# One half of the scores copied by VectorE in five steps of a batch (attention with mixed heads, then a Fourier mixer)

## Chip, core and metric

The program runs on one core of a Trainium2 chip. The core has TensorE (PE in the profile; its weight loads are PEld), VectorE (DVE), ScalarE (ACT), GpSimd (POOL) and SyncE (SP, which here only issues DMA transfers). The metric is the time of the whole program on the device, in microseconds; the median of the runs is used.

## The reference

Two blocks follow each other, all in float32. Only the first is touched by the change, the second is named because its work goes on beside it.

```python
scores = scale * np.matmul(q, k.transpose(0, 1, 3, 2))      # 8 batches, 12 heads, 448 x 448
scores = np.einsum('bhij,hg->bgij', scores, w_pre)          # heads mixed
attn = np.exp(scores - max) / (sum + 1e-09)                 # softmax over j
attn = np.einsum('bhij,hg->bgij', attn, w_post)             # heads mixed again
x = np.matmul(attn, v)                                      # then (B, H, S, D) -> (B, S, H*D)
u = x + np.real(np.fft.fft(np.fft.fft(x, axis=1), axis=2))
un = (u - mean) / sqrt(var + 1e-06)
out = u + np.maximum(un @ w_ch1, 0.0) @ w_ch2
```

## The kernel before

The program has a mixing stage (attention and the Fourier transforms, `mix_phase`) and a feed-forward stage (`ffn_phase`), which starts while the last batch's transforms are still being done.

**Steps.** The mixing stage is a software pipeline of 184 steps, 23 for each of the 8 batches (`GS`). A batch's 448 query rows are cut into 8 blocks of two or three steps (`BLOCKS`). A step mixes and normalises 20 query rows for all 12 heads. For the step two ahead it runs the premix on TensorE (`emit_premix`, L656, into the two `mx` banks), row maxima on VectorE (L663), two exponentials on ScalarE (L670), sums and reciprocals on VectorE (L677, L678) and a scaling on GpSimd (L680). For the step itself it runs the postmix on TensorE (L690) and a transpose on VectorE (L703).

**Products beside the steps.** These are due at fixed steps, given by tables at the top of the file:
- `emit_qk` (L628): the scores of two heads (of rows x = 0 and 1) for one block, into two `ms` banks. Six slices make up a block's tile `Sb`. Due by `AT_QK`.
- `emit_av` (L720): attention times v, two `ms` banks.
- "full" products: `emit_xpose` (L601; here also called a turn: seven transposes of q or k, four into one `ms` bank and three into the next), `emit_x` (L764, transposes of the result X, two banks), `emit_z` (L829) and `emit_s2` (L845), the two passes of the Fourier transform, one bank each. The last one is followed by four additions on VectorE (L856, L858) that read its bank.

All of them share four `ms` banks in strict rotation. A bank is free again once it has been copied into SBUF. These copies all go through one helper (`copy`, L489), which picks ScalarE for "a" and VectorE for "d". For scores the table says `"QK": "aa"`, both halves by ScalarE; only the first two blocks of the first batch have `"ad"`.

**Order.** Each engine's instruction order in this stage is written out by hand for TensorE, VectorE, ScalarE and GpSimd (`manual_schedule`). Within a step it follows `ORDERS`, alternating:

```python
"pre post flush AV max0 exp0 QK max1 exp1 turn scale conv full gather"
"pre post flush max0 max1 QK exp0 AV turn exp1 scale conv gather full flush"
```

A product puts its copies on a list `pend`; they are written into the queues at the next `flush`, and every "full" product begins with one (`take`). So the score copies of a step that has a full product come, on each engine, behind that step's `exp1`, `scale` and `conv`. `conv` is one weight-conversion operation on VectorE (`wts.deal(1)`, lines 250 to 310), a chore that prepares the feed-forward weights from step 4 on.

A gather (L645) then collects twelve heads' rows for a step out of `Sb` into `Kr`. It is issued by SP, waits for the block's last score copy, and is due five steps ahead of its step. `Sb` has two buffers, so the first score copy of a block waits until the gathers of the block before the last are done.

**Steps that matter below**, counted within a batch (step number modulo 23), with what TensorE does behind the scores there: step 0 (L845, then L764), step 2 (a second pair of scores, then L845), step 5 (L764, then a turn of q), step 13 (L764, then a turn of q), step 15 (a turn of q, then a turn of k). In step 5, 13 and 15 the turns belong to the next batch, so the last batch has none; there VectorE has statistics for the feed-forward stage in their place.

Of the kernel before, what the change touches and what calls it, by code (L numbers as in the profile page):

```python
# [43 lines left out]
NBL = len(BLOCKS)  # L44
BLOCK_AT = [sum(k[2] for k in BLOCKS[:n]) for n in range(NBL + 1)]
GS = BLOCK_AT[-1]
# [47 lines left out]
AT_QK = ((0, 2, 1), (0, 1, 2), (0, 1, 2), (1, 2, 2),  # L94
         (0, 1, 2), (0, 1, 2), (0, 1, 2), (0, 1, 2))
AT_AV = ((1, 2, 4), (0, 1, 3), (1, 3, 5), (1, 3, 4))
AT_X = ((13, 0), (23, 1), (28, 3), (29, 2))
AT_Z = (39, 40, 40, 42)
AT_S = ((42, 44), (46, 48))
# [7 lines left out]
ENG = {("tr", "q", 4): "d", ("tr", "q", 3): "a", ("tr", "k", 4): "a",  # L107
       ("tr", "k", 3): "d", "QK": "aa", "AV": "aa", "X": "aa", "z": "a"}
# [342 lines left out]
def mix_phase(ctx, tc, rest, ident, q, k, v, w_pre, w_post, u_scr, u_rev, wts, lead):  # L451
# [36 lines left out]
    def copy(eng, out, in_):  # L488
        (nc.scalar.copy if eng == "a" else nc.vector.tensor_copy)(out=out, in_=in_)  # L489
# [11 lines left out]
    def ms_tile():  # L501
        return ms[-1]()
# [54 lines left out]
    def emit_load_qk(b, xx, nm, y):  # L557

        src = q if nm == "q" else k
        if y == 0 and b == 0 and xx == START[-1]:  # L560

            if "raw" not in first:
                first["raw"] = ppv.tile([P, GT, 2 * S], F32, name="Pv", tag="Pv")
            batches[b]["raw" + nm, xx] = first["raw"][:, nm == "q"].rearrange(
                "p (c x d) -> p c x d", c=C7, x=2)
        elif y == 0:
            batches[b]["raw" + nm, xx] = praw.tile([P, C7, 2, D], F32, name="raw" + nm,
                                                   tag="raw")
        t = batches[b]["raw" + nm, xx]
        for x in range(2):  # L570
            eng = nc.gpsimd if b else (nc.sync, nc.scalar if xx == START[0] else nc.gpsimd)[x]
            eng.dma_start(
                out=t[64 * y:64 * y + 64, :, x, :],
                in_=src[b, 6 * y + 2 * xx + x].rearrange("(p c) d -> p c d", c=C7))
        return True

    def emit_load_v(b, pr, y):
        if y == 0:
            batches[b]["v", pr] = pvv.tile([P, 2, C7 * D], F32, name="vv", tag=f"vv{pr}")
        h = 6 * y + 2 * pr  # L580
        nc.gpsimd.dma_start(
            out=batches[b]["v", pr][64 * y:64 * y + 64, :, :],
            in_=v[b, h:h + 2].rearrange("h (p c) d -> p h (c d)", c=C7))


    def emit_xpose(b, xx, nm):
        st = batches[b]
        raw = st.pop(("raw" + nm, xx))
        w = WQ if nm == "q" else S
        t = pqt.tile([P, 2, w], F32, name=nm + "T", tag=nm + "T")  # L590
        st[nm + "T", xx] = t
        rt = _row(t)
        if nm == "q":
            eng = nc.gpsimd if b else nc.vector
            eng.memset(t[:, :, 0:MG], 0.0)
            eng.memset(t[:, :, MG + S:WQ], 0.0)
        evs = []
        for c0, n in ((0, 4), (4, 3)):
            ps = ms_tile()
            for c in range(n):  # L600
                nc.tensor.transpose(  # L601
                    ps[:, c * P:(c + 1) * P],
                    raw[:, c0 + c].rearrange("p x d -> p (x d)"), ident[:, :])
            if nm == "q":
                dst = _ap(t, MG + c0, [[rt, P], [1, n], [WQ, 2], [C7, 64]])
                src = ps[:, :n * P].rearrange("p (c y t) -> p c y t", c=n, y=2)
            else:
                dst = _ap(t, 32 * c0, [[rt, P], [32, n], [HS, 4], [1, 32]])
                src = ps[:, :n * P].rearrange("p (c y t) -> p c y t", c=n, y=4)
            evs.append(lambda dst=dst, src=src, n=n: copy(ENG["tr", nm, n], dst, src))  # L610
        return evs

    def emit_qk(n, xx):

        bk = blocks[n]
        st = batches[bk["b"]]
        engs = ENG["QK"] if n > 1 else "ad"
        if "Sb" not in bk:
            bk["Sb"] = psb.tile([P, 6, S], F32, name="Sb", tag="Sb")
        c0, w = bk["r0"] + MG, R * bk["rs"]  # L620
        n = 64 + w
        pss = [ms_tile() for _ in range(2)]
        for y in range(2):
            for o in (64 * y, 64 * y + 32):
                lo = c0 + o - 64 + (0 if y else w)
                hi = min(lo + 32, c0 + w)
                for x in range(2):
                    nc.tensor.matmul(  # L628
                        pss[x][o:o + hi - lo, :S],
                        st["qT", xx][64 * x:64 * x + 64, y, lo:hi],  # L630
                        st["kT", xx][64 * x:64 * x + 64, y, :],
                        start=True, stop=True)
        return [lambda x=x: copy(engs[x], bk["Sb"][:n, 2 * xx + x, :],
                                 pss[x][:n, :S]) for x in range(2)]
# [250 lines left out]
    def due(kind, at, fn):  # L885
        fill[kind].append((at, len(fill[kind]), fn))
# [4 lines left out]
    for b in range(B):  # L891
        f = b * GS
        at_t = [(a, nm, xx) for xx, at in enumerate(AT_T) for nm, a in zip("qk", at)]
        if b == 0:

            for i, xx in enumerate(START):
                for j, nm in enumerate("kq"):
                    for y in range(2):
                        due("none", -40, lambda xx=xx, nm=nm, y=y: emit_load_qk(0, xx, nm, y))
                    due("full", 2 * i + j - 20, lambda xx=xx, nm=nm: emit_xpose(0, xx, nm))  # L900
                for n, at in enumerate((2 * i - 18, i - 13)):
                    due("QK", at, lambda n=n, xx=xx: (emit_qk(n, xx), n))
            for pr in range(3):
                for y in range(2):
                    due("none", -40, lambda pr=pr, y=y: emit_load_v(0, pr, y))
        else:
            for at, (a, nm, xx) in zip(AT_L if b > 1 else AT_L1, sorted(at_t, key=lambda e: e[0])):
                for y in range(2):
                    due("none", f + at[y] - GS if b > 1 else at[y],
                        lambda b=b, xx=xx, nm=nm, y=y: emit_load_qk(b, xx, nm, y))  # L910
            for xx, at in enumerate(AT_T):
                for nm, a in zip("qk", at):
                    due("full", f + a - GS,
                        lambda b=b, xx=xx, nm=nm: emit_xpose(b, xx, nm))
        for pr in range(3 if b else 0):
            for y in range(2):
                due("none", f + AT_V[pr][y], lambda b=b, pr=pr, y=y: emit_load_v(b, pr, y))
        for n in range(0 if b else 2, NBL):
            for xx in range(3):
                due("QK", AT_QK0[n][xx] if b == 0 and n in AT_QK0 else  # L920
                    f + BLOCK_AT[n] - 8 + AT_QK[n][xx],
                    lambda n=NBL * b + n, xx=xx: (emit_qk(n, xx), n))
        for n in range(NG):
            for pr in range(3):
                due("AV", f + GROUP_AT[n + 1] + AT_AV[n][pr],
                    lambda a=b * NG + n, pr=pr: (emit_av(a, pr), None))
            at, gi = AT_X[n]
            if b == B - 1 and n > 1:
                at += 2
            due("full", f + at, lambda g=groups[b * NG + gi]: emit_x(g))  # L930
        for n, at in enumerate(AT_Z):
            due("full", f + at, lambda b=b, n=n: emit_z(b, n // 2, n % 2))
        for pair in range(2):
            for par in range(2):
                due("full", f + AT_S[pair][par],
                    lambda b=b, pair=pair, par=par: emit_s2(b, pair, par))
# [19 lines left out]
    def take(kind, s):  # L956
        large = 0
        while fill[kind] and fill[kind][0][0] <= s:
            fn = fill[kind].pop(0)[2]
            if kind == "none":  # L960
                large += bool(fn())
            elif kind == "full":
                flush()
                pend.extend((1, e, None) for e in fn())
            else:
                room(2)
                evs, n = fn()
                pend.extend((1, e, n) for e in evs)
        return large
# [3 lines left out]
    with tc.manual_schedule(engines={ET.PE, ET.DVE, ET.Activation, ET.Pool}):  # L973
        while s <= TOT - GS + AT_X[-1][0]:
            old = len(later)
            n = take("none", s)
# [577 lines left out]
```

## Time and profile before

| what | value |
|---|---|
| median of 3 runs | 2299.19 us (2297.72 to 2299.28) |
| profiled execution | 2299.42 us, its span 2297.6 us |
| granted TensorE clock | 0.998 |
| premix L656 on TensorE | 2944 matmuls, 192.2 us |
| scores L628 on TensorE | 3072 matmuls, 191.6 us |
| attention times v, L720 | 5376 matmuls, 160.8 us |
| maxima L663 on VectorE | 368, 618 ns each |
| transposes L703 on VectorE | 184, 1107 ns each |
| exponentials L670 on ScalarE | 368, 631 ns each |

The page counts busy time per engine, then follows the chain that ended last back from the last instruction. The mixing stage fills roughly the first 800 us. Every copy of a bank into SBUF has the line L489, whoever makes it, so copies are told apart by tile and engine: `Sb<-ms` is a score copy, `qT<-ms` and `kT<-ms` those of a turn, `X<-ms` those of L764, `XT<-ms` those of L720. In a timeline the columns are start, duration (both us), engine, line, operation, tiles, shapes and count; in brackets the idle time before it and what ended it. Copies in a row on one engine overlap a little, so two of them take less than twice the time of one.

### The profile page before, as it was taken

The page shows a single profiled execution, that of the slowest core. Times are in us where ns is not written, and L with a number is a line of the kernel's source. Part 1 is how long each engine was busy: PE and PEld are TensorE (multiplying, and loading weights), DVE is VectorE, ACT ScalarE, POOL GpSimd, SP SyncE. Part 2 cuts the span into 40 slices and gives each one's busy share as a digit, 9 for nine tenths or more (in the row PEclk, how much of TensorE's full clock was granted, in tenths as well). Part 3 has the DMA queues.
Part 4 walks back from the last instruction along what each step waited for, and adds up shares of the span by engine and source line. Part 5 has one row for each costly group of instructions (what it writes and reads, how often), then busy time and mean ns, then how long its engine had stood idle before and what let it go on. Part 6 is the DMA issues. An engine that isn't in the chain of part 4 may idle for free.

```text
span 2297.6 us, 60793 instructions
## 1 busy us (share of the span) xinstructions
PE 2249.2 (98%) x22894; PEld 1740.7 (76%) x22894; DVE 1711.2 (74%) x3640; ACT 1167.1 (51%) x3330; POOL 1292.1 (56%) x1805
## 2 busy tenths in 40 slices
PE   7999999999999999999999999999999999999998
PEld 3455555555554677777899999999999899999998
DVE  5778787888877757776877787778778777765545
ACT  4676767767676533231445445444444445434434
POOL 7677878879768541221555555546555645454334
PEclk9999999999999999999999999999999999999999
DMA  7566565666756475649677887788787987795664
GB/s 185 168 178 181 168 192 171 190 179 181 202 151 190 143 265 182 230 162 327 191 181 180 252 214 184 212 195 242 204 197 184 277 188 174 191 257 121 143 146 76
DMA packets 228063, 439.45 MB, mean 191 GB/s; under 512 B 35964, under 2 KB 149558, under 8 KB 227772
## 3 DMA queue, kind: packets, MB, share of 16 engines
q1 hardware_dynamic: 156620, 301.52, 38.2%
q0 software_dynamic: 68864, 133.00, 30.4%
q8 instruction: 183, 3.00, 0.6%
q10 hardware_dynamic: 2288, 1.05, 0.2%
q14 instruction: 108, 0.88, 0.1%
HBM read 213.16 MB, written 143.16 MB: 155 GB/s over the span
## 4 chain that ended last, share of the span: by engine, by line
PE 87%; DVE 5%; DMA 3%; ACT 2%; issue 1%; POOL 1%; SPq 1%; ACTq 0%; DVEq 0%; POOLq 0%
PE psP L1213 18%; PE psP L1335 14%; PE psR L1213 9%; PE psR L1335 7%; PE mx L656 6%; PE ms L720 6%; PE ms L628 5%; PE po L690 5%; PE psQ L1213 4%; PE psQ L1335 3%; PE psP L1290 3%; PE ms L845 2%; PE ms L601 2%; DMA Kr<-Sb 1%; PE psR L1290 1%
## 5 line engine op out<-in xcount | busy, mean ns | idle before, releaser
L1369 POOL DMA_DIRECT2D out_dram<-od x172 | 209.1, 1276 | 261.7 <-DVE od L1357 175.3
L680 POOL TENSOR_SCALAR PP<-PP,rcp 128x448 f32<-128x448 f32 x368 | 234.6, 647 | 170.2 <-DVE rcp L678 123.8
L670 ACT ACTIVATE PP<-mx,nmx 128x448 f32<-128x448 f32 x368 | 230.2, 631 | 165.2 <-DVE nmx L663 157.2
L663 DVE TENSOR_REDUCE nmx<-mx 128x1 f32<-128x448 f32 x368 | 212.5, 618 | 101.2 <-PE mx L656 99.1
L1176 POOL TENSOR_TENSOR hq<-h 128x128 f32<-128x128 f32 (+1 forms) x210 | 130.0, 619 | 255.9 <-ACT h L1235 122.3
L1363 ACT COPY od<-psP 128x192 f32<-128x192 f32 x488 | 156.1, 320 | 172.0 <-PE psP L1335 170.6
L1366 DVE TENSOR_TENSOR od<-od 128x768 f32<-128x768 f32 x210 | 201.3, 972 | 52.7 <-ACT od L1363 52.3
L703 DVE STREAM_TRANSPOSE Pv<-po 128x896 f32<-128x896 f32 x184 | 203.7, 1107 | 2.9 <-PE po L690 2.1
L489 ACT COPY Sb<-ms 124x448 f32<-124x448 f32 (+1 forms) x378 | 181.7, 540 | 46.0 <-PE ms L628 19.2
L656 PE MATMUL mx<-Kr,kw 60*32 60x448 f32 x2944 | 192.2, 549 | 4.3 <-ACT PP L670 2.3
L628 PE MATMUL ms<-kT,qT 64*32 64x448 f32 (+1 forms) x3072 | 191.6, 545 | 3.9 <-ACT qT L489 2.8
L720 PEld LDWEIGHTS ms<-Pv,vv 64*64 64x64 f32 x5376 | 138.1, 132 | 73.7 <-issue 48.8
L690 PE MATMUL po<-PP,kw 60*32 60x448 f32 x2944 | 184.0, 537 | 1.2 <-POOL PP L680 1.1
L1213 PE MATMUL psP<-qs,w1t 128*128 128x256 f32 x744 | 179.2, 380 | 2.4 <-DVE h L1234 1.5
L1213 PE MATMUL psP<-ks,w1t 128*128 128x256 f32 x744 | 179.3, 380 | 0.4 <-DVE h L1234 0.3
L720 PE MATMUL ms<-Pv,vv 64*64 64x120 f32 (+1 forms) x5376 | 160.8, 263 | 3.6 <-ACT Sb L489 2.2
L254 POOL TENSOR_SCALAR wst<-wst 128x256 f32<-128x256 f32 (+1 forms) x76 | 118.6, 1569 | 67.2 <-ACT wst L265 66.9
L1213 PEld LDWEIGHTS psP<-qs,w1t 128*128 128x128 f32 x744 | 139.5, 190 | 19.4 <-DVE h L1234 1.9
L1213 PEld LDWEIGHTS psP<-ks,w1t 128*128 128x128 f32 x744 | 139.5, 190 | 17.2 <-DVE h L1234 0.7
L1213 PE MATMUL psP<-ub,w1t 128*128 128x256 f32 x528 | 127.2, 379 | 1.1 <-DVE h L1234 1.1
L1234 DVE TENSOR_TENSOR h<-h,psP 128x512 f32<-128x512 f32 x42 | 28.8, 686 | 127.9 <-PE psP L1213 112.3
L1335 PE MATMUL psP<-w2t,hq 128*128 128x192 f32 x490 | 122.5, 332 | 1.2 <-DVE od L1357 1.2
(199 smaller groups left out, 5301.6 us busy)
## 6 DMA issues: line engine op xcount, KB each, us to landing
Kr<-Sb SPq DMA_DIRECT2D x730, 105.0 KB
out_dram<-od POOLq DMA_DIRECT2D x172, 384.0 KB, 6.3
qs<-ub SPq DMA_DIRECT2D x89, 384.0 KB
ks<-ub SPq DMA_DIRECT2D x88, 384.0 KB
ub<-ub SPq DMA_DIRECT2D x79, 384.0 KB
w1t<-w SPq DMA_DIRECT2D x42, 384.0 KB
w2t<-w SPq DMA_DIRECT2D x42, 384.0 KB
raw<-in_moe_w_ch_dram SPq DMA_DIRECT2D x32, 384.0 KB
```

The source lines that it names most:

```text
L628: nc.tensor.matmul(pss[x][o:o + hi - lo, :S], st["qT", xx][64 * x:64 * x + 64, y, lo:hi], st["kT", xx][64 * x:64 * x + 64, y, :], start=Tr ...
L656: nc.tensor.matmul(mx[x][64 * z + o:64 * z + o + 32, :S], kw1[64 * x:64 * x + KR, o:o + 32], Kr[64 * x:64 * x + KR, z, :], start=True, sto ...
L663: nc.vector.tensor_reduce(nmx[:, :], steps[T]["mx"][x][:, :S], axis=AX.X, op=ALU.max, negate=True)
L670: nc.scalar.activation(steps[T]["PP"][:, x, :], steps[T]["mx"][x][:, :S], ACTF.Exp, bias=steps[T]["nmx", x][:, :], accum_out=steps[T]["den ...
L680: nc.gpsimd.tensor_scalar(PP[:, x, :], PP[:, x, :], rcp[:, x:x + 1], 1.0, op0=ALU.mult, op1=ALU.mult)
L690: nc.tensor.matmul(po[o:o + 32, z, :S], kw2[64 * z:64 * z + KR, y, :], PP[64 * z:64 * z + KR, :, c * HS:(c + 1) * HS], start=True, stop=True)
L703: nc.vector.transpose(turned[a]["Pv"][:, j, :].rearrange("p (z s) -> p z s", z=2), steps[T]["po"][:, :, :S])
L720: nc.tensor.matmul(pss[y][64 * x:64 * x + 64, :nu * R], st["v", pr][64 * y:64 * y + 64, x, jb * D:(jb + 1) * D], _ap(Pv, 64 * y * rp + 32 ...
L1213: mm = nc.tensor.matmul(p[:, m, :], w1[i][:, kc, m * P:(m + 1) * P], ub[:, kc, :], start=i in (0, 4, 1)[:3 - seed] and m == kc == 0, stop= ...
L1335: nc.tensor.matmul(ps[j, key][:, :DQ], a, b, start=m in (0, 4), stop=True, skip_group_check=True)
L1366: eng.tensor_tensor(D[j][:, :, :], D[j][:, :, :], D[k][:, :, :], op=ALU.add)
L1369: nc.gpsimd.dma_start(out=acc[t, r, d], in_=D[j][:, :, :], accum_op=ALU.add)
```

## The change

In the steps 0, 2, 5, 13 and 15 of a batch (`TWO`), the second of the two score copies (x = 1) is put on VectorE. The step is worked out from the tables where the product is made due, and handed to `emit_qk`. The first batch's blocks 0 and 1 keep what they had. Step 2 makes two score products, so it has two such copies; the other steps have one. Nothing else is edited.

```diff
+TWO = (0, 2, 5, 13, 15)
...
-    def emit_qk(n, xx):
+    def emit_qk(n, xx, at=None):
...
-        engs = ENG["QK"] if n > 1 else "ad"
+        engs = "ad" if n < 2 or at in TWO else ENG["QK"]
...
             for xx in range(3):
                 due("QK", AT_QK0[n][xx] if b == 0 and n in AT_QK0 else
                     f + BLOCK_AT[n] - 8 + AT_QK[n][xx],
-                    lambda n=NBL * b + n, xx=xx: (emit_qk(n, xx), n))
+                    lambda n=NBL * b + n, xx=xx, at=(BLOCK_AT[n] - 8 + AT_QK[n][xx]) % GS:
+                    (emit_qk(n, xx, at), n))
```

## The prediction

> **What bounds the kernel now.** I read the page first, then the view of one source line (L489, the helper that makes every bank copy), then the waits of the mixing stage, and last the timeline of one changed step.
>
> ```profile
> PE 2249.2 (98%) x22894; PEld 1740.7 (76%) x22894; DVE 1711.2 (74%) x3640; ACT 1167.1 (51%) x3330; POOL 1292.1 (56%) x1805
> ...
> PE 87%; DVE 5%; DMA 3%; ACT 2%; issue 1%; POOL 1%; SPq 1%; ACTq 0%; DVEq 0%; POOLq 0%
> ```
>
> TensorE bounds it: 87% of the chain that ended last. VectorE is the next busiest (74%), ScalarE has half its time free. Time is won or lost only where a bank copy makes TensorE wait, so the copies come next:
>
> ```profile
> L489 ACT COPY Sb<-ms x378: 524/538/610, 13.0 to 758.9; 124x448 f32<-124x448 f32 x165, 104x448 f32<-104x448 f32 x24
> ...
> L489 DVE COPY Sb<-ms x6: 625/625/625, 13.0 to 27.2; 124x448 f32<-124x448 f32 x6
> ...
>   PE ms L601: 7.3, 20
> ```
>
> A score copy takes 0.54 us on ScalarE and 0.625 us on VectorE. The last line is from the list of who waited for the copies: TensorE's turns of q and k (L601) stood still for 7.3 us in 20 places. The waits from 100 to 800 us add the other kind:
>
> ```profile
> PE ms L845 <- ACT Sb L489: 2.7, 6, 0.6
> ```
>
> So at most about 10 us of TensorE's time hang on score copies in the changed steps. Which half of the copies ends these waits is seen in step 5 of batch 5:
>
> ```profile
> 531.12 1.10 DVE L703 STREAM_TRANSPOSE Pv<-po 128x896 f32<-128x896 f32 x1
> ...
> 531.90 0.20 ACT L670 ACTIVATION_READ_ACCUMULATOR PP<-mx,nmx 128x1 f32 x1
> 532.00 0.96 ACT L489 COPY Sb<-ms 124x448 f32<-124x448 f32 x2
> 532.11 0.99 POOL L790 TENSOR_TENSOR xs<-xs 113x383 f32<-113x383 f32 x1
> 532.21 0.16 DVE L677 TENSOR_REDUCE rcp<-den 128x2 f32<-128x4 f32 x1
> 532.40 0.17 DVE L678 RECIPROCAL rcp<-rcp 128x2 f32<-128x2 f32 x1
> 532.48 1.04 DVE L297 TENSOR_TENSOR wst<-wst,tmp 128x384 f32<-128x384 f32 x1
> ...
> 532.58 0.99 PE L601 MATMUL ms<-ident,rawq 128*128 128x128 f32 x7 [0.60 <-ACT Sb L489]
> ...
> 533.45 1.12 DVE L489 COPY qT<-ms 128x512 f32<-128x512 f32 x1
> 533.49 0.98 PE L656 MATMUL mx<-Kr,kw 60*32 60x448 f32 x16
> ```
>
> Single records give the rest: ScalarE's first copy runs from 532.00 to 532.52, the second ends at 532.96. With four banks in rotation, X (L764) takes the two that the scores don't hold, and the turn needs the scores' banks: four transposes into the first half's, three into the second half's. The turn starts 0.05 us after the FIRST copy ends; its fifth transpose follows 0.50 us later (533.08) without a stop. The wait is for the first copy, which comes right after the two exponentials. The second is never waited for.
>
> [...]
>
> **The change part by part.** 47 copies (39 of 124 rows, 8 of 104) leave ScalarE for VectorE; the comparison of the instruction orders shows nothing else moved on TensorE, ScalarE or GpSimd. Removed: 47 x 0.43 us (the distance of two copies in a row on ScalarE) = 20 us of an engine that is half idle. Added: 47 x some 0.54 us = 25 us on VectorE. The new copy goes behind the reciprocal and behind the weight chore (the "conv" entry; L297 above), in front of the turn's own VectorE copy. TensorE's fifth transpose now waits for VectorE instead of ScalarE; the first four wait for ScalarE's first copy as before, which moves nowhere.
>
> The cost of each turn is then: end of the chore + 0.54 us (VectorE instructions start about 0.08 us before the last one's end, 0.625 - 0.08) + 0.05 us (from a copy's end to TensorE's start, as above), less the time at which the fifth transpose started. Chore end / fifth transpose, in us, by batch:
> Step 5, batches 1 to 6: 147.12/146.93, 245.70/245.13, 342.19/341.75, 438.01/437.31, 533.52/533.08, 628.15/628.03. Late by 0.78 + 1.16 + 1.03 + 1.29 + 1.03 + 0.71 = 6.0.
> Step 13, batches 0 to 6: 88.88/89.19, 179.96/179.47, 277.15/277.47, 372.29/372.61, 469.01/468.84, 563.91/563.94, 659.58/659.64. Late by 0.28 + 1.08 + 0.27 + 0.27 + 0.76 + 0.56 + 0.53 = 3.8.
> Step 15, batches 0 to 6 without 3: 97.19/97.50, 188.56/188.05, 285.62/285.77, 477.15/477.14, 572.19/572.24, 667.69/667.94. Late by 0.28 + 1.10 + 0.44 + 0.60 + 0.54 + 0.34 = 3.3. In batch 3 the first copy itself waited for a gather until 380.88, when VectorE was free: nothing. Step 5 of batch 0 finds free banks: nothing. Batch 7 has no turns.
> Sum 13.1 us over 19 turns, all on TensorE's path: the next premix (L656) is right behind the turn.
>
> Step 0: the products behind (L845, then X) take the two free banks and the first copy's; no wait on VectorE. But the new copy stands ahead of the four additions (L856, L858) that free L845's bank, and step 1's first product needs it. In batches 4 to 7 they start 0.31, 0.29, 0.44 and 0.46 us later; against where L628 or L720 started (417.52, 512.82, 607.79, 703.61) that is 0.24 + 0.07 + 0.35 + 0.25 = 0.9 us.
> Step 2: two copies go, but L845 takes the bank of the first, which stays on ScalarE: its wait of 2.7 us stays. The two new ones end at 520.53 in batch 5, when VectorE idles until 520.62 for L845: hidden.
>
> VectorE's later start on the turn's copies does not come through: in batch 5 after step 5 they end at about 535.1, and the next maximum, which waits 1.0 us after the premix's start, is due at 534.52 + 1.0 = 535.5. On SP's queue the gather of a block waits for its last copy: in step 5 from 532.98 to about 534.1, but TensorE is 1.0 us later there itself, so the distance holds; in step 2 by 0.25 us, with three steps left until the premix that needs it. One store of u per batch goes one gather (0.8 us) later, with no one waiting for its tile then.
>
> Sum: 13.1 + 0.9 = 14.0 us. I take off 1 us for places where TensorE waits longer for other reasons than a turn's normal 0.23 us (gathers that arrive late, as in step 15 of batch 3): they can swallow a delay made shortly before. That leaves +13.0. The profiled execution took 2299.42 us (span 2297.6), hence 2312.4; its distance to the median 2299.19 is 0.2, hence 2312.2, taken as 2312.
>
> Bounds of what the trace does not show. A copy behind a chore may start earlier (the turn's k copy ends 0.39 us behind the q copy for 384 columns, so 0.45 for 448): 19 x 0.09 = 1.7 us less. From VectorE's end to TensorE's start may be 0.1 us: 1 us more. Swallowed: 0 to 4 us. Together +9 to +16.
>
> **Rivals.**
> 1. Forecast: the second half waits behind the chore; 2312 (2308 to 2316). For it: program order and the times above. 0.78.
> 2. Faster: ScalarE, freed of 0.43 us, gives back the waits of L601 and L845, 7.3 + 2.7 = 10 us: 2289. For it: these waits are put down to its score copies, and ScalarE's work in a step ends late. Against it: they end with the first copy. It decides if the first copy, or the exponentials ahead of it, came some 0.2 us earlier in most steps, and chores shrank to under 0.3 us so that nothing was given back. 0.06.
> 3. No change: later waits for gathers swallow most, say 11 of 14 us: 2302. Against it: such waits beyond the normal are about 4 us in the trace. 0.07.
> 4. Slower still: VectorE's extra 25 us push maxima and exponentials into the next premix, or late gathers hold up ScalarE's first copy of a block (it sat 18.6 us for gathers in 9 places). If half of the 25 us showed beside a part of the 14: 2320. Against it: room of 0.4 us and more in the steps worked above. 0.09.
>
> **How the numbers follow.** A difference under 0.2% (4.6 us) can't be told from none. Slower: 0.78 + 0.09, less a little for a forecast that is nearly swallowed: 0.86. Same: rival 3, 0.07. Faster: 0.07. The range: cases 1 and 4 up to 2319, down to 2304.
>
> **What would show it.** In the profile after, the fifth transpose of the turns in steps 5, 13 and 15 waits for "DVE Sb" for 0.3 to 1.3 us, some 13 us in all; waits of L601's first transpose on ScalarE stay near 0.23 us each; VectorE holds 53 score copies at about 625 ns; the premixes behind are late by as much and nothing makes it up. Wrong it would be if those transposes don't wait for VectorE, or if the mixing stage ends less than 5 us later.

## The result, and the profile after

| | before | after |
|---|---|---|
| median, measured side by side (6 runs each) | 2299.24 us (2292.60 to 2300.12) | 2312.61 us (2309.16 to 2317.68) |
| profiled execution, its span | 2299.42, 2297.6 us | 2309.16, 2307.4 us |
| score copies on ScalarE, on VectorE | 378, 6 | 331, 53 |
| mixing stage ends (last copy of L720's banks) | 798.0 us | 811.2 us |

The ratio is 1.0061, 95% interval 1.0048 to 1.0074: the changed kernel is slower, by 13.4 us as the difference of the medians. The profiled execution of the changed kernel is its fastest of six, so the two profiles lie only 9.8 us apart; the section on the prediction comes back to this. In the changed kernel a line of before has moved by 1, behind the step function by 2: L489 is now L490, L601 is L602, L764 is L765, and so on.

The engines' busy time and the engines' shares of the chain that ended last, from the page of the changed kernel:

```profile
PE 2251.6 (98%) x22894; PEld 1738.9 (75%) x22894; DVE 1732.6 (75%) x3687; ACT 1149.3 (50%) x3283; POOL 1291.0 (56%) x1805
...
PE 88%; DVE 5%; DMA 3%; ACT 1%; issue 1%; SPq 1%; POOL 1%; DVEq 0%; ACTq 0%; POOLq 0%
```

TensorE does the same work: 2251.6 us busy after 2249.2. VectorE has 21 us more, ScalarE 18 us less, and neither bounds the program. Of the 9.8 us between the two profiles, 7.4 are time in which TensorE stands, 2.4 come from its busy time. The view of the copies' line shows where it stands:

```profile
L490 ACT COPY Sb<-ms x331: 523/532/587, 13.3 to 772.3; 124x448 f32<-124x448 f32 x142, 104x448 f32<-104x448 f32 x24
L490 DVEq EVENT_SEMAPHORE  x158: 49/50/50, 41.4 to 768.2; - x158
...
L490 DVE COPY Sb<-ms x53: 604/623/626, 13.3 to 768.3; 124x448 f32<-124x448 f32 x45, 104x448 f32<-104x448 f32 x8
...
  PE ms L602: 15.6, 37
```

The columns of the first three are count, shortest, median and longest duration in ns, first and last start in us. The last line is from the list of who waited for these copies: 15.6 us in 37 places where the kernel before had 7.3 us in 20. I had not counted on the second line; it matters in the third experiment. The waits from 100 to 800 us split TensorE's standing by what ended it:

```profile
PE ms L602 <- DVE Sb L490: 10.2, 18, 1.1
PE ms L602 <- ACT Sb L490: 4.5, 15, 0.8
PE ms L846 <- ACT Sb L490: 2.3, 6, 0.7
```

The first line is new. The waits for ScalarE's first copy (second line; 6.5 us in 17 places before) and the wait of step 2 (third line; 2.7 us before) stayed about as they were. Step 5 of batch 5 once more, now in the changed kernel:

```profile
538.86 0.53 ACT L490 COPY Sb<-ms 124x448 f32<-124x448 f32 x1
...
539.27 0.17 DVE L679 RECIPROCAL rcp<-rcp 128x2 f32<-128x2 f32 x1
...
539.35 1.02 DVE L298 TENSOR_TENSOR wst<-wst,tmp 128x384 f32<-128x384 f32 x1
...
539.45 0.66 PE L602 MATMUL ms<-ident,rawq 128*128 128x128 f32 x4 [0.39 <-ACT Sb L490]
...
540.29 0.61 DVE L490 COPY Sb<-ms 124x448 f32<-124x448 f32 x1
...
540.96 0.55 PE L602 MATMUL ms<-ident,rawq 128*128 128x128 f32 x3 [0.85 <-DVE Sb L490]
```

ScalarE's one copy ends at 539.39 and the turn starts 0.05 us later, as before. Then the seven transposes, one group of before, are cut in two: the fifth comes at 540.96, 1.51 us after the first instead of 0.50. It waits for VectorE's copy, which started 0.08 us before the chore (L298) ended; from the copy's end to the transpose it is 0.06 us. (The bracket says 0.85 because it counts from the modelled end of the fourth transpose; that, and the two turns ahead of 100 us, is why the 10.2 us of the view above are less than the sum below.)

This distance from the first transpose to the fifth can be read from single records for every turn. From step 0 on it is 0.49 us in nearly every turn of the kernel before (0.44 to 0.52; the six turns ahead of step 0, at the start of the program, have 0.85 to 0.91). In the changed kernel it is 1.25, 1.65, 1.52, 1.77, 1.51, 1.69 in step 5 (batches 1 to 6), 0.91 in four turns of step 13 and 1.33, 1.06, 1.03 in the others, and 0.90 to 1.59 in step 15. Less 0.49 each, 20 turns are late by 6.45 + 3.63 + 3.93 = 14.0 us.

### The profile page after: what moved, and what is told of

It is laid out like the page before. It is cut to its first block, busy times and chain, and to the rows that moved or that the text cites. A ratio compares the mean times of both kernels' runs of the same rounds, so it can differ in the third digit from the quotient of the medians.

```text
span 2307.4 us, 60928 instructions
## 1 busy us (share of the span) xinstructions
PE 2251.6 (98%) x22894; PEld 1738.9 (75%) x22894; DVE 1732.6 (75%) x3687; ACT 1149.3 (50%) x3283; POOL 1291.0 (56%) x1805
## 4 chain that ended last, share of the span: by engine, by line
PE 88%; DVE 5%; DMA 3%; ACT 1%; issue 1%; SPq 1%; POOL 1%; DVEq 0%; ACTq 0%; POOLq 0%
PE psP L1215 18%; PE psP L1337 14%; PE psR L1215 9%; PE psR L1337 7%; PE mx L657 6%; PE ms L721 6%; PE ms L629 5%; PE po L691 5%; PE psQ L1215 4%; PE psQ L1337 3%; PE psP L1292 3%; DMA Kr<-Sb 2%; PE ms L846 2%; PE psR L1292 1%; PE ms L830 1%
## 5 line engine op out<-in xcount | busy, mean ns | idle before, releaser
L704 DVE STREAM_TRANSPOSE Pv<-po 128x896 f32<-128x896 f32 x184 | 203.5, 1106 | 2.7 <-PE po L691 1.8
L490 ACT COPY Sb<-ms 124x448 f32<-124x448 f32 (+1 forms) x331 | 161.5, 537 | 37.4 <-PE ms L629 19.0
```

Source lines behind the costliest of these rows:

```text
L704: nc.vector.transpose(turned[a]["Pv"][:, j, :].rearrange("p (z s) -> p z s", z=2), steps[T]["po"][:, :, :S])
```

## The experiments

Each kernel is the changed one with the edit shown, and was timed in five rounds beside the kernel before on the same chip. Differences are ratios less one, times the median of before in that session (2297.35 us in the first four, 2296.61 us in the last three); they can lie a microsecond or two from the difference of the two medians.

Theory A: the second half's copy is late because of what VectorE does in front of it, and the turn's fifth transpose waits for it. Theory B: the cost is the extra work on VectorE, 25 us, wherever it stands.

### 1 and 2: the turn steps alone, the other steps alone

```diff
-TWO = (0, 2, 5, 13, 15)
+TWO = (5, 13, 15)
```

> Steps 5, 13 and 15 alone: the 23 copies that stand in front of a turn of q or k (L602 here). Theory A (TensorE's fifth transpose waits for a copy that stands behind the weight chore on VectorE): nearly all of the loss, +13 to +14 us, 2312 to 2313. Theory B (25 us more work on VectorE, wherever it is put): 23 of 47 copies, about half the loss, +6 to +7 us, 2306.

Measured: 2309.91 us, ratio 1.0060 (1.0041 to 1.0079): 13.8 us more by the ratio.

```diff
-TWO = (0, 2, 5, 13, 15)
+TWO = (0, 2)
```

> Steps 0 and 2 alone: the other 24 copies. Theory A: they free banks that no product waits for soon; only the additions behind step 0 come later, +0 to +1 us, 2299 to 2300. Theory B: the other half, +6 to +7 us, 2306.

Measured: 2299.56 us, ratio 1.0013 (1.0006 to 1.0021): 3.0 us more.

Steps 0 and 2 have over half of the moved copies (24 of 47) and bring 3 us; steps 5, 13 and 15 have the other 23 and bring all the rest. What they have and the others lack is a turn behind the scores. Theory B, which wanted the time split like the copies, falls. The 3 us of the other steps are more than the 0 to 1 that A gave them; the interval ends at 1.4 us below. Where they arise was not traced.

### 3: the copy in front of the chore

```diff
-    "QK max1 exp1 turn scale conv full gather",
+    "QK max1 exp1 turn scale flush conv full gather",
...
-    "AV turn exp1 scale conv gather full flush"))
+    "AV turn exp1 scale flush conv gather full flush"))
```

The order of the other engines' arithmetic is unchanged; on VectorE the copy now stands between the reciprocal and the chore.

> All 47 copies as in the changed kernel, but a flush in front of the weight chore, so that VectorE makes the copy first and the chore after it; the orders of TensorE, ScalarE and GpSimd stay. Theory A: the copy ends some 0.54 us after the reciprocal, about 0.09 us after the fifth transpose would have started: 19 x 0.09 = 1.7, and 0.9 for step 0 stays: +2 to +3 us, 2302. Theory B (the work itself): no change against the changed kernel, +13 us, 2312.

Measured: 2309.91 us, ratio 1.0063 (1.0044 to 1.0083): 14.5 us more. A's number was missed by over 11 us. The timeline of this kernel, same step:

```profile
539.20 0.17 DVE L679 RECIPROCAL rcp<-rcp 128x2 f32<-128x2 f32 x1
...
539.37 0.66 PE L602 MATMUL ms<-ident,rawq 128*128 128x128 f32 x4 [0.59 <-ACT Sb L490]
539.60 0.62 DVE L490 COPY Sb<-ms 124x448 f32<-124x448 f32 x1 [0.23 <-DMA Kr<-Sb]
...
540.27 0.55 PE L602 MATMUL ms<-ident,rawq 128*128 128x128 f32 x3 [0.25 <-DVE Sb L490]
```

The chore is gone from in front of the copy, and the fifth transpose comes 0.90 us after the first instead of 1.51. It ought to have come at some 0.58. The bracket of the third line has the missing part: VectorE stood for 0.23 us between the reciprocal and its copy, where in the kernel before the instruction behind the reciprocal starts 0.08 or 0.09 us ahead of its end in 164 of 184 steps. The bracket names a gather; but 37 of the 38 copies of this kernel that are led by four queue instructions as below have a gap of 0.23 or 0.24 us, which gathers that happened to be late would not give. Single records of VectorE's queue show what filled the gap (start and end in us, the semaphores waited for by number):

```
539.195 539.361 DVE   RECIPROCAL       118
539.209 539.259 DVEq  EVENT_SEMAPHORE  112 111
539.306 539.356 DVEq  EVENT_SEMAPHORE  113 110
539.404 539.453 DVEq  EVENT_SEMAPHORE  114 101
539.501 539.551 DVEq  EVENT_SEMAPHORE  115 100
539.595 540.219 DVE   COPY Sb<-ms      116
```

The copy is the first VectorE instruction to write into this `Sb` buffer since eight transfers read it, so it has eight DMA semaphores to wait for beside TensorE's. Four queue instructions of 0.05 us, 0.1 us apart, take two of them each, and the copy starts 0.04 us after the last. The first begins 0.01 us after the reciprocal, which itself has to wait for the sums in front of it (semaphore 118). In the changed kernel the four also begin right with the reciprocal (at 539.29, the reciprocal at 539.27) and are over at 539.63; the chore runs until 540.37, so there they cost nothing. With nothing else in front, each turn is late by 0.41 us. (ScalarE's queue has four or five such instructions, of 0.04 us, in front of its own first copy of 48 of the 64 blocks before, and none in front of the copy that follows it.) The turns of this kernel in steps 5, 13 and 15 show 0.90 or 0.91, all but one (step 5 of batch 6, 0.47): 19 x 0.41 = 7.8 us. Theory A had taken the copy to start as soon as the reciprocal was done.

This leaves some 7 us of the 14.5, whose interval runs from 10 to 19. In the profiled execution the premixes behind steps 3 and 4 come 2.1 and 1.3 us later in sum than before, counted from the second batch on. I have no experiment for these; they stay open.

### 4: the first half on VectorE, not the second

```diff
-TWO = (0, 2, 5, 13, 15)
+TWO = (5, 13, 15)
...
-        engs = "ad" if n < 2 or at in TWO else ENG["QK"]
+        engs = "ad" if n < 2 else "da" if at in TWO else ENG["QK"]
```

> Steps 5, 13 and 15, but the FIRST half of the scores goes to VectorE (behind the chore, as in the changed kernel) and the second stays on ScalarE. Theory A: the turn's first transpose waits for the chore and the copy, so each of 19 turns loses 0.49 us more than with the second half: +13.5 + 9.3 = +23 us, 2322. A rival by which TensorE waits for whichever copy ends last, or for the whole tile: as with the second half, +13 us, 2312.

Measured: 2308.68 us, ratio 1.0052 (1.0033 to 1.0071): 11.9 us more, and the turn looks as in the first experiment: the first four transposes go with ScalarE's copy, the fifth is late, by 0.42 us and more. A's number was missed, for a premise of it doesn't hold. The section on the kernel says that the `ms` banks go round in strict rotation, and they don't: where each product goes is settled when the program is built, and differs from kernel to kernel. Here the turn's first tile got the bank of ScalarE's copy, though that was now the second half: in step 5 of batch 5, the built program has VectorE's half in bank 4 and ScalarE's in bank 5, and the turn writes 5 first and 4 second. So this run doesn't tell what a late first half costs. The rival, by which TensorE waits for the copy that ends last, had the number and not the mechanism: the first four transposes don't wait for VectorE's copy. It shows that "first four behind the first half" was true of the two kernels compared and isn't a rule.

### 5: the copy right behind the transpose

```diff
-    "QK max1 exp1 turn scale conv full gather",
+    "QK max1 exp1 turn flush scale conv full gather",
...
-    "AV turn exp1 scale conv gather full flush"))
+    "AV turn exp1 flush scale conv gather full flush"))
```

All five steps again. The copy stands between the transpose of the mixed scores (L704) and the sums and reciprocal, so that its queue instructions have time to pass before VectorE comes to it.

> All 47 copies stay on VectorE, but stand right behind the transpose of the mixed scores (L704), in front of the reciprocal and the weight chore. Theory A (the delay is what VectorE does between the transpose and the copy's end: chore, reciprocal, and 0.31 us for the copy's many semaphore waits, which e3 showed bare): the waits pass under the transpose, the copy ends near 532.8 on the clock of the timeline of before where the fifth transpose starts at 533.08, so no turn is late: fifth transpose 0.49 us after the first in steps 5, 13 and 15, at most 1 us left from step 0, 0 to +3 us in all. Reciprocal and scaling come 0.54 us later; by the timeline of before they have some 0.7 us of room in step 5. Theory B (the delay is the extra 25 us of work on VectorE, wherever it stands, as e3's +12.6 could be read): +8 to +13 us again.

Measured: 2298.30 us, ratio 1.0011 (1.0003 to 1.0019): 2.5 us more. The timeline of this kernel, same step:

```profile
530.68 1.10 DVE L704 STREAM_TRANSPOSE Pv<-po 128x896 f32<-128x896 f32 x1
...
531.56 0.53 ACT L490 COPY Sb<-ms 124x448 f32<-124x448 f32 x1
...
531.71 0.58 DVE L490 COPY Sb<-ms 124x448 f32<-124x448 f32 x1
...
532.14 0.98 PE L602 MATMUL ms<-ident,rawq 128*128 128x128 f32 x7 [0.59 <-ACT Sb L490]
532.22 0.13 DVE L678 TENSOR_REDUCE rcp<-den 128x2 f32<-128x4 f32 x1
```

The seven transposes are one group again. VectorE's copy starts 0.07 us before the transpose ends, with no gap, and is over at 532.29, before the fifth transpose at 532.63 needs the bank. The four queue instructions did not run under the transpose, as the expectation had it: their records lie between 530.09 and 530.44, before it began. The fifth comes at 0.49 in every turn of these steps (0.47 to 0.50). All 47 copies are on VectorE as in the changed kernel, and some 11 of its 13 us are gone: the cost was the place in the order, which also decides whether the copy's waits show. Reciprocal and scaling come half a microsecond later, and the room that the expectation named covers them.

### 6: fewer waits on the copy

```diff
-TWO = (0, 2, 5, 13, 15)
+TWO = (0, 2, 4, 5, 12, 13, 15)
```

and the edit of experiment 3. Now VectorE's first write to a block's buffer is the one in step 4 or 12, and the copies of steps 5 and 13 have only TensorE to wait for.

> e3 (copy in front of the chore) with VectorE also taking one half in steps 4 and 12: the copy that first touches a block's buffer then stands there, and the copies of steps 5 and 13 wait for TensorE alone; that of step 15 keeps its eight DMA waits. Theory A with the semaphore waits as the cause of e3's remainder: fifth transpose at 0.55 to 0.65 us after the first in steps 5 and 13 (12 and 13 turns less one or two), still 0.90 in step 15; against e3 12 to 13 times 0.3 us = 3 to 4 us less, so +8 to +10 us against before, if the copies in steps 4 and 12 cost nothing. If the 0.4 us are something else (the way from VectorE's copy to TensorE, or the copy's own start): 0.90 in all three steps and +12 to +13.

Measured: 2311.85 us, ratio 1.0072 (1.0055 to 1.0088): 16.5 us more. The two statements of the expectation came apart. The turns did as theory A said:

```profile
540.15 0.17 DVE L679 RECIPROCAL rcp<-rcp 128x2 f32<-128x2 f32 x1
...
540.23 0.60 DVE L490 COPY Sb<-ms 124x448 f32<-124x448 f32 x1
540.32 0.88 PEld L602 LDWEIGHTS ms<-ident,rawq 128*128 128x128 f32 x7 [0.79 <-ACT Sb L490]
540.33 1.11 PE L602 MATMUL ms<-ident,rawq 128*128 128x128 f32 x7 [0.59 <-ACT Sb L490]
```

The copy starts 0.08 us before the reciprocal ends, and the fifth transpose comes at 0.56 to 0.61 in steps 5 and 13 (0.47 in the one turn that was not late in experiment 3) instead of 0.90. Step 5 of the first batch shows 0.95: there the copy with the DMA waits falls into the same step. In step 15, which kept its DMA waits, it is 0.90 or 0.91, except where the turn itself was late (0.57 in batch 3). The waits' price is 0.33 us a copy, shown in one kernel with and without them.

But the total did not fall (12.6 to 20.2 us more than before, experiment 3 10.1 to 19.1), for the copies in steps 4 and 12 were not free. Step 12 of batch 4:

```profile
469.95 0.62 DVE L490 COPY Sb<-ms 124x448 f32<-124x448 f32 x1 [2.29 <-DMA Kr<-Sb]
469.96 0.53 ACT L490 COPY Sb<-ms 124x448 f32<-124x448 f32 x1 [2.18 <-DMA Kr<-Sb]
...
472.52 1.10 DVE L704 STREAM_TRANSPOSE Pv<-po 128x896 f32<-128x896 f32 x1
473.40 0.53 ACT L490 COPY Sb<-ms 124x448 f32<-124x448 f32 x1
...
473.98 1.11 PE L602 MATMUL ms<-ident,rawq 128*128 128x128 f32 x7 [2.53 <-ACT Sb L490]
```

A late gather used to hold up ScalarE alone at this point (1.59 us in experiment 3). Now VectorE stands with it, for 2.29 us, and with it the maxima, the transpose and the exponentials of the next step; TensorE stands for 2.53 us before the turn of step 13 (0.80 in experiment 3). From the second batch on the premixes behind step 13 lose 6.4 us in sum against before (2.1 us in experiment 3).

### 7: the copy in front of the transpose

```diff
-TWO = (0, 2, 5, 13, 15)
+TWO = (5, 13, 15)
...
-        engs = "ad" if n < 2 or at in TWO else ENG["QK"]
+        engs = "ad" if n < 2 else "da" if at in TWO else ENG["QK"]
...
                 elif op in ("post", "turn"):
+                    if op == "turn" and s > 5 and s % GS in TWO and pend:
+                        pend.pop(0)[1]()
```

> Only steps 5, 13 and 15; the first half goes to VectorE and is copied in front of the transpose of the mixed scores (L704), the second to ScalarE behind the exponentials. By the waits in the built program the turn's first four transposes still wait for ScalarE's copy and the fifth for VectorE's, which is then over half a microsecond early. Theory A: no turn is late (0.49 us), the transpose L704 and the reciprocal come some 0.6 us later; 0 to +3 us if the next postmix doesn't wait for the scaling, up to 19 times 0.3 = +6 us if it does. Theory B (extra VectorE work as such): +8 us or more.

Measured: 2301.20 us, ratio 1.0022 (1.0014 to 1.0030): 5.1 us more, inside what A gave. No turn is late (0.49 or 0.50 in all), but the transpose and all behind it are: in step 5 of batch 5 the copy runs from 531.27 and the transpose starts at 531.81. That the 5 us come from there is argued, not isolated. In front of the transpose the copy pushes the step's own work; behind it, as in experiment 5, only the reciprocal.

No version beats the kernel before. Experiment 5 is the nearest, and 0.03% to 0.19% above it. The built program deals the banks anew in each kernel; this was not varied by itself.

## Why the prediction was right, point by point

The forecast was 2312.0 us within 2304 to 2319; 2312.6 was measured. The likeliest case was the one that happened.

- **Which wait decides.** The prediction said that the first transpose goes on waiting for ScalarE's first copy, which moves nowhere, and the fifth waits for VectorE. Both are in the timeline after. Experiment 1 puts the cost in the steps with a turn, experiment 5 takes it away by moving the same copies.
- **The turns' sum.** Worked out 6.0 + 3.8 + 3.3 = 13.1 us; measured 6.45 + 3.63 + 3.93 = 14.0. It is this close partly because errors met. A chore's length isn't its own: in step 13 of batch 1 the chore (128x256 elements) took 1.08 us before and 0.27 us after, so 1.08 us were counted and 0.42 came; in step 5 of batch 6 it took 0.67 before and 1.19 after, so 0.71 were counted and 1.20 came. In the profile before, the length goes with what GpSimd does beside it. Of the chores of this shape with one input (TENSOR_SCALAR, uint32) in the mixing stage before, the 20 that begin with GpSimd idle take 0.27 or 0.28 us; the four that begin while one of its two-input operations (TENSOR_TENSOR, such as L790) runs take 0.30 to 1.10 us, and each ends 0.15 or 0.16 us after that operation does. And no short chore gave less than 0.41, where the prediction had 0.27 to 0.34: the queue instructions of the copy follow the reciprocal, and a chore that is over before the last of them doesn't count. Experiment 3, with no chore in front, has the same 0.41. The prediction priced the copy by duration and knew nothing of its waits; this term was missing. The floor of 20 x 0.41 makes 8.2 us of the 14.0; what long chores add to it is 5.8.
- **Nothing in step 15 of batch 3.** Wrong: 0 was expected because the first copy had waited for a gather there. After, the first copy held the turn up by only 0.16 us, VectorE was not free that early, and the turn was late by 0.42.
- **Step 0.** Worked out 0.9 us; the premixes behind step 1 come later by 0.90 us in sum from the second batch on. That the sums agree is luck. The prediction had 0.07, 0.35 and 0.25 us in batches 5 to 7, and there nothing came (0.01 us at most); batch 4 has 0.26 for 0.24, and 0.76 us lie in batch 2, where none was forecast. Its reason doesn't hold either: in both built programs the first product of step 1 takes the bank of the second half of the scores and that of the first half of X, not the bank of L845, so it doesn't wait for the additions. Step 2 was priced at nothing; experiment 2, both steps together, measured 3.0 (1.4 to 4.8).
- **What is swallowed.** 1 us was taken off; the profile has more. In step 11 of the first batch, before any turn is late, the premix comes 0.6 us later than before; the last premix comes 13.5 us later. Of the 12.9 us between, the turns' lateness makes 14.0. Another part has nothing to do with the copies: from 742.7 to 746.1 us TensorE's granted clock is 0.50 in this execution and TensorE is busy all the time, an estimate of 1.7 us from these figures; before, no such stretch lies in the mixing stage after 36.3 us. So about 2.8 us were swallowed on balance, within the 0 to 4 of the bounds. Part of it can be seen: in step 0 of batch 2, TensorE stood in the midst of L845 before and not after, which gives back 1.3 us by itself.
- **How close the total is.** The mixing stage ends 13.2 us later, but the feed-forward stage of this execution is 3.4 us shorter than in the profile before. So 14.0 us of late turns belong to an execution that took 9.8 us longer than the one before, and 13.4 us is a difference of medians. The sum and the median agree to a microsecond in part by chance; what carries the explanation is the wait in each turn and the experiments 1, 2 and 5.
- **The rivals.** ScalarE's freed time gave little back: 4.5 us of waits for its copies in the turns remain of 6.5, and those of L846 are 2.3 of 2.7, together 2.4 us where rival 2 had 10. VectorE's extra work as such costs at most what experiment 5 has left, 2.5 us (0.7 to 4.4). That the new copy keeps its place in VectorE's queue is borne out by the timelines: in step 5 of batch 5 of the changed kernel TensorE's scores are done at 538.22 us and the copy's queue instructions at 539.63, and it starts at 540.29, as the chore written in front of it ends (540.37); experiment 5 depends on this.

## What to carry to other kernels

Before a copy is given to another engine, look at what stands between its earliest start and its place in that engine's queue, and who waits for it; the duration on the new engine was the smaller part here (0.62 us against 0.53, where the turns came 0.41 to 1.28 us late). Count its waits too: here the first VectorE write into a buffer had to wait for the eight transfers that had read it, and this showed (0.33 us) where VectorE had nothing else to do between the reciprocal and the copy. Either put such a copy where the engine has other work until the waits have passed, or leave that first write to the engine that does it already. If such a wait can be long, as for the gather of experiment 6 (2.29 us), what stands behind it on the new engine is held up as well. And don't take a bank from the order of the source: look into the built program for whose bank a product gets.

## What the runs showed that I had not expected

- A VectorE copy with nine semaphores to wait for is led by four queue instructions, 0.05 us each and 0.1 us apart. With only the sums and the reciprocal in front it starts 0.23 us after the end of the reciprocal, instead of 0.08 us before it (experiment 3 against 6). It is the queue that needs the time and not the instruction right in front: behind a chore of a microsecond, or behind maximum and transpose as in experiment 5, where the four are over before the transpose begins, nothing shows.
- The same copy of 448 columns took 0.58 us (median 585 ns) right behind the transpose and 0.62 us (624 ns) in front of the chore. No run here tells why.
